# One load for the first keys, two banks for the last output tile, 28 accumulating transfers instead of 26, and all steps in a new order

## The chip, the core and the metric

The kernel runs on one core of one Trainium2 chip. A core has four engines that compute: TensorE (PE, matrix products; its weight loads are listed as PEld), VectorE (DVE), ScalarE (ACT) and GpSimd (POOL). SyncE (SP) only issues transfers. Each engine works through its own queue in the order of the program and waits on semaphores for the others. Transfers between memory and the core, and inside it, run on 16 DMA engines; they are issued here from SP's, ACT's and POOL's queues. The matrix products write into PSUM, eight banks of 128 x 512 floats; everything else lies in SBUF.

The metric is the device time of one execution in microseconds (us), as the median of several runs.

## The reference

Two stages. The first is attention without a softmax, for 4 batches of 4 heads, 1088 positions and a head size of 32. Queries and keys go through a feature map: two small matrices S1 and S2 give 8 numbers each, and the 64 products of these are the features. The second stage takes the 4352 rows of 128 numbers through a hidden layer of 2048 with a rational function in place of a usual activation.

```python
def phi(x):
    a = np.einsum('rd,bhsd->bhsr', S1, x)
    b = np.einsum('rd,bhsd->bhsr', S2, x)
    return np.einsum('bhsi,bhsj->bhsij', a, b).reshape(*x.shape[:-1], r * r)
q_p, k_p = (phi(q), phi(k))
kv = np.einsum('bhsf,bhsd->bhfd', k_p, v)
z = np.sum(k_p, axis=2)
num = np.einsum('bhsf,bhfd->bhsd', q_p, kv)
den = np.einsum('bhsf,bhf->bhs', q_p, z)[..., None] + 1e-06
x = (num / den)                    # then [B, S, H*D] as 4352 rows of 128
h = x @ w_in
P = a[0] + a[1] * h + a[2] * h2 + a[3] * h3      # h2 = h*h, h3 = h2*h
Q = 1.0 + np.abs(b[0]) * np.abs(h) + np.abs(b[1]) * h2
g = P / (Q + 1e-06)
out = g @ w_out
```

## The kernel before

The work is cut into steps, and the string `ORDER` (lines 38 to 76) lists all 650 of them by name. The loop at line 728 emits them in that order, so each engine's queue holds its share of the steps in that order and nothing is moved later. A step that stands earlier in the string than it needs to only matters on its own queue. A last letter of a step names the engine where there is a choice: `a` is ACT, `d` is DVE.

**Attention.** `I0` to `I11` (function `early`) are first loads, from SP's queue: in the kernel before, `I0` and `I1` bring the first batch's keys in two halves, `I11` brings S2, `I2` and `I7` the queries, `I3` the values, `I8` the coefficients, `I4` to `I6` w_in, `I9` and `I10` w_out. `F1.k`, `F1.q`, `F1.v` and so on load the next batches into the same buffers. `SS0` makes the sketch weights from S1 and S2 on DVE and POOL. `Kb` is the key part of batch b: `T0` to `T2` transposes on DVE, `s` sketches on PE, `c` a copy of them out of PSUM, `f` the features on DVE, `p` the products with the values on PE, `k` the copy of the result ("kvz"). `Qb.y` is chunk y of the queries of batch b: `T` transpose (DVE), `sk` sketch (PE), `c` copy, `dw` and `dr` a way through memory that repeats the sketches over the partitions (SP), `f` features (DVE), `p` products (PE), `pl` the denominator plus 1e-6, `r` reciprocal (DVE), `x` quotient (DVE), `b` transpose back (PE), `kk` copy into xT, the input of the second stage.

**Second stage.** 21 units, listed in `UNITS`, each some tokens by some of the 16 hidden blocks; most are 512 tokens by 8 blocks, which is a tile of 128 x 4096. Unit i has these steps: `H` h = w_in x on PE (line 518), in parts of 1024 columns into two wide PSUM buffers; `E` copies a part into SBUF as bf16 (line 272 on ACT); `U` takes |h| (DVE, line 531), `W` multiplies by |b1| and adds |b0| (line 539), `Y` multiplies by |h| (line 554). `L` and `X` on ACT make r = 1/Q as the exponential of minus a logarithm (lines 576 and 581). `P` is a3 h + a2 on DVE (line 559) or ACT (line 562), `V` multiplies it by h (line 572), `S` is s = h r (line 585), `G` multiplies the two (line 589). `Or`, `Os`, `Og` add r, s and g times the scaled w_out into the output tile in PSUM (line 618), each 32 products of 128 x 128 for a full unit: the constant, the linear and the higher terms of P. `ST` copies a finished output tile to SBUF, `OUT` stores it from SP's queue. The output copies have two buffers, so an `ST` needs the store of the tile two before it to have read.

Two lists change a unit's work. In units of `SQ`, ACT squares h (`D`) and an accumulating transfer from POOL's queue adds |h| to it in SBUF (`M`, line 550, two transfers of 2048 columns). In units of `TWO`, the linear coefficient is added to g by two accumulating transfers from POOL's queue (`A`, line 568, between `V` and `G`), and `Os` is left out. Units of `FOUR` (16 and 17) form the square and the cube on DVE (`B`, `C`) and have gathers `Om` and `On` in place of `Og`. `Zn` are n products of a zero tile that nobody reads, to keep PE at work.

**PSUM.** Three banks `att_ps` serve the attention, two buffers of two banks each serve `H`, and one bank, `out_ps`, holds the output tile (line 607). The first gather of a tile therefore needs the copy of the tile before to be done. The last tile, tokens 4096 to 4351, lies in one bank; its halves are copied by DVE (line 633) and by ACT (line 635) and stored from SP's and ACT's queues.

Of the kernel before, what the change touches and what calls it, by code (L numbers as in the profile page):

```python
# [43 lines left out]
Q0.1.b K1.p0 K1.p1 E2.1.a Q1.0.c.a w5.a Q0.1.kk.a L0.0 P2.0.d Q0.2.f Q0.2.p Q0.2.pl.a K1.k0.a X0.0 Q1.2.T U2.0.d
Q0.2.r Q1.1.sk Q1.2.sk Q0.3.dw F2.k Q1.0.dw Q0.2.x Q0.2.b Or0.0 W2.0.d S0.0 V2.0 K2.T0 G0.0 Y2.0 Q0.2.kk.a L1.0
Q1.1.c.a X1.0 H3.0 E3.0.a H3.1 E3.1.a K2.s0 K2.c0.a H3.2 L2.0 Q1.2.c.a E3.2.a F2.q Q0.3.dr Q1.1.dw S1.0 K2.T1 P3.0.d
G1.0 Q2.0.T K2.f0 Q2.1.T H3.3 E3.3.a Q0.3.f U3.0.d K2.T2 W3.0.d Q2.2.T Y3.0 Os0.0 H4.0 H4.1 Og0.0 Q2.0.sk Q1.0.dr
Q1.2.dw Q1.1.dr K2.s1 Q0.3.p X2.0 E4.0.a P3.1.a H4.2 Q0.3.pl.d K2.c1.d Q1.0.f Q2.0.c.a E4.1.a Og1.0 Q0.3.r V3.0 Q1.0.p
Q0.3.x L3.0 Q1.0.pl.a Q1.2.dr H4.3 E4.2.a Os1.0 Q1.0.r E4.3.a Q1.0.x Q0.3.b Q0.3.kk.a Q1.0.b Or2.0 S2.0 U4.0.d
Q1.0.kk.a H5.2 K2.f1 Q1.1.f W4.0.d X3.0 Q2.0.dw H5.3 E5.3.a G2.0 Q2.1.sk F2.v Q2.2.sk Q2.1.c.a F3.q E5.2.a Q1.1.p Y4.0  # L50
Q2.2.c.a Q1.1.pl.a Q1.1.r H5.0 E5.0.a Og2.0 L4.0 H5.1 Q1.2.f Or1.0 H6.2 Q1.1.x S3.0 E5.1.a Os2.0 ST2.a E6.2.a P4.0.d
Q3.1.T H6.3 Q1.1.b E6.3.a X4.0 Q1.1.kk.a H6.0 E6.0.a U5.0.d H6.1 Q3.0.T Q3.0.sk Q2.1.dw Q3.0.c.a W5.0.d E6.1.a K2.p0
K2.p1 K2.k0.a D6.0 Q1.2.p V4.0 Y5.0 S4.0 F3.k K3.T2 K3.T1 H7.0 K3.T0 E7.0.a U6.0.d G3.0 M6.0 Q1.2.pl.a Os4.0 H7.2
Or4.0 L5.0 E7.2.a H7.3 Q2.0.dr Q2.0.f Q2.0.p Q1.2.r Q2.1.dr Q2.1.f Q3.0.dw Q1.2.x X5.0 P5.0.d Q3.0.dr Q2.2.dw Q1.2.b
Q1.2.kk.a E7.3.a H7.1 Og3.0 G4.0 Q2.0.pl.d Q3.2.T E7.1.a Q2.0.r H8.3 V5.0 Q2.0.x Q2.0.b S5.0 L6.0 H8.2 E8.2.a U7.0.d
E8.3.a F3.v Or3.0 Q2.0.kk.a P6.0.d W7.0.d P7.0.d H8.0 V6.0 Os3.0 X6.0 Y7.0 E8.0.a S6.0 H8.1 E8.1.a U8.0.d D8.0 Q2.2.dr
OUT2 Og4.0 ST4.a H9.0 Q3.1.sk Q3.1.c.d Q2.2.f Q2.1.p Q2.1.pl.d K3.s0 K3.c0.d Q2.1.r Q3.2.sk Q3.2.c.d E9.0.a H9.1 Or6.0
L7.0 M8.0 Q2.1.x Q2.1.b K3.f0 H9.2 E9.1.a X7.0 E9.2.a Os6.0 H9.3 E9.3.a V7.0 AW0 Or5.0 P8.0.d H10.3 G6.0 L8.0 G5.0
S7.0 U9.0.d E10.3.a W9.0.d H10.0 E10.0.a V8.0 Q3.1.dw Y9.0 Og6.0 X8.0 H10.1 H10.2 Og5.0 E10.1.a A7.0 G7.0 E10.2.a
Q2.1.kk.a H11.0 Q3.1.dr Q3.1.f Os5.0 S8.0 D10.0 Q2.2.p E11.0.a U10.0.d P9.0.d K3.s1 Q2.2.pl.d ST6.a Q3.2.dw H11.1  # L60
Or8.0 Q3.0.f OUT6 Q2.2.r H11.2 K3.c1.d Q2.2.x L9.0 E11.1.a P10.0.d Q2.2.b K3.f1 V9.0 M10.0 V10.0 X9.0 E11.2.a H11.3
E11.3.a S9.0 K3.p0 K3.p1 w7.d U11.0.d w6.d L10.0 W11.0.d H12.1 E12.1.a Or7.0 H12.0 K3.k0.d Q3.0.p Q3.1.p X10.0 Y11.0
Q3.1.pl.d H12.2 Q3.0.pl.a G8.0 E12.0.a L11.0 E12.2.a Q3.0.r Os8.0 A9.0 H12.3 E12.3.a Q3.1.r Og8.0 Q3.0.x Q3.0.b Og7.0
Q3.1.x G9.0 Q2.2.kk.a S10.0 A10.0 Q3.0.kk.d H13.0 D12.0 Q3.1.b Q3.1.kk.a U12.0.d ST8.a M12.0 P12.0.d H13.1 E13.1.a
Q3.2.dr P11.0.d E13.0.a Or9.0 X11.0 H13.3 Q3.2.f V12.0 G10.0 V11.0 S11.0 H13.2 E13.3.a E13.2.a U13.0.d Or10.0 H14.1
E14.1.d L12.0 OUT4 Q3.2.p W13.0.d Q3.2.pl.a Q3.2.r H14.2 E14.2.d H14.0 X12.0 E14.0.a H14.3 Q3.2.x Q3.2.b Y13.0 E14.3.a
Q3.2.kk.a H15.2 D14.0 S12.0 U14.0.d A12.0 G12.0 E15.2.a Og10.0 Og9.0 ST10.a P14.0.d Z4 H15.3 P13.0.d L13.0 A11.0
Or12.0 G11.0 V14.0 V13.0 E15.3.a X13.0 S13.0 H15.1 Og11.0 E15.1.a H15.0 E15.0.a Or11.0 M14.0 U15.0.d L14.0 H16.1
# [11 lines left out]
def kernel(  # L80
# [61 lines left out]
    def spread_s(eng, i, s_in):  # L142
        t = consts.tile([128, D], FP, name=f"s_raw{i}")
        eng.dma_start(out=t, in_=bass.AP(tensor=s_in.tensor, offset=s_in.offset, ap=[[0, 16], [D, R], [1, D]]))
# [626 lines left out]
```

## Time and profile before

| | |
|---|---|
| median of 3 runs | 254.69 us (254.11 to 255.16) |
| the profiled execution | 254.41 us, span 252.6 us from first to last instruction |
| outside the span | 1.8 us |
| PE, DVE, ACT, POOL busy | 244.7, 240.3, 229.2, 31.2 us |
| granted TensorE clock | 1.00 |

The profile lists when each instruction of each engine started and how long it took, and for each idle time of an engine which event ended it. The busy share is an average over the span; the view by windows cuts it into stretches. Instructions on one engine overlap at their ends by up to about 0.1 us (a product of 128 x 4096 is listed with 2.28 us, and the next starts 2.20 us after it), and the ends of matrix products are modelled, so a PE that is listed as busy need not be at its peak.

### The profile page before, as it was taken

The numbers are of one execution on the slowest core, as the hardware profiler recorded it, in microseconds if no ns is written. First come the engines' busy times: TensorE is split into PE (matmuls) and PEld (weight loads), VectorE is DVE, ScalarE is ACT, GpSimd is POOL, SyncE is SP. The second block draws the span as 40 slices with busy tenths as digits, with TensorE's granted clock in tenths as the row PEclk, the third lists the DMA queues.
The fourth block names the chain that finished last, engine by engine and source line by source line (L and its number), as shares of the span: only waits on it lengthen the run. The fifth ranks groups of instructions, "written<-read, shape, count | busy, mean of one in ns | idle before, by whom it ended". The sixth has DMA issues, their size and how long they took to land.

```text
span 252.6 us, 6102 instructions
## 1 busy us (share of the span) xinstructions
PE 244.7 (97%) x2606; PEld 171.9 (68%) x2606; DVE 240.3 (95%) x231; ACT 229.2 (91%) x177; POOL 31.2 (12%) x59
## 2 busy tenths in 40 slices
...
GB/s 164 277 328 210 126 241 197 131 100 257 174 20 156 188 195 77 87 197 192 4 42 168 180 236 79 115 190 195 44 197 57 200 210 91 29 16 3 42 23 21
DMA packets 22458, 34.47 MB, mean 136 GB/s; under 512 B 2976, under 2 KB 14880, under 8 KB 22432
## 3 DMA queue, kind: packets, MB, share of 16 engines
...
## 4 chain that ended last, share of the span: by engine, by line
DVE 45%; PE 33%; issue 11%; DMA 6%; ACT 2%; SPq 1%; POOL 0%; DVEq 0%; ACTq 0%
PE h_ps L518 18%; PE out_ps L618 9%; DVE g L589 7%; DVE g L572 7%; DVE w L554 5%; DVE s L585 5%; DVE u L531 4%; DMA w<-u 4%; DVE g L559 4%; DVE w L539 3%; DMA v_sb<-in_v_dram 2%; PE att_ps L433 2%; DVE g L594 2%; PE att_ps L337 2%; DVE a_all L417 1%
## 5 line engine op out<-in xcount | busy, mean ns | idle before, releaser
L518 PE MATMUL h_ps<-xT,w_in_sb 128*128 128x512 f32 (+1 forms) x320 | 128.7, 539 | 0.1
L518 PEld LDWEIGHTS h_ps<-xT,w_in_sb 128*128 128x128 f32 x320 | 56.7, 190 | 36.6 <-issue 31.8
L272 ACT CAST hh<-h_ps 128x1024 bf16<-128x1024 f32 x66 | 66.6, 1047 | 3.3 <-PE h_ps L518 2.8
L581 ACT ACTIVATE r<-ln 128x4096 bf16<-128x4096 f32 (+2 forms) x21 | 63.1, 3005 | 0.4 <-ACT xT L272 0.3
L576 ACT ACTIVATE ln<-w 128x4096 f32<-128x4096 bf16 (+2 forms) x16 | 45.0, 2811 | 0.4 <-DVE w L554 0.4
L585 DVE TENSOR_TENSOR s<-hh,r 128x4096 bf16<-128x4096 bf16 (+2 forms) x21 | 39.5, 1881 | 0.0
L618 PEld LDWEIGHTS <-r 128*128 128x128 bf16 x544 | 31.8, 98 | 8.9 <-issue 8.6
L618 PEld LDWEIGHTS <-g 128*128 128x128 bf16 x544 | 31.6, 98 | 6.9 <-issue 6.0
L618 PE MATMUL out_ps<-w_out,r 128*128 128x128 bf16 x544 | 33.6, 219 | 1.2 <-ACT out_sb L272 1.1
L589 DVE TENSOR_TENSOR g<-g,s 128x4096 bf16<-128x4096 bf16 (+2 forms) x19 | 34.7, 1835 | 0.0
L572 DVE TENSOR_TENSOR g<-g,hh 128x4096 bf16<-128x4096 bf16 (+2 forms) x19 | 34.6, 1829 | 0.0
L618 PE MATMUL out_ps<-w_out,g 128*128 128x128 bf16 x480 | 29.7, 219 | 0.0
L554 DVE TENSOR_TENSOR w<-w,u 128x4096 bf16<-128x4096 bf16 (+2 forms) x16 | 28.0, 1750 | 0.0
L550 POOL DMA_DIRECT2D w<-u x10 | 9.3, 1026 | 131.0 <-ACT w L544 111.6
L618 PEld LDWEIGHTS <-s 128*128 128x128 bf16 x352 | 20.6, 98 | 4.7 <-issue 4.6
L531 DVE TENSOR_SCALAR u<-hh 128x4096 uint16<-128x4096 uint16 (+2 forms) x21 | 21.4, 1020 | 0.8 <-ACT hh L272 0.8
L568 POOL DMA_DIRECT2D g<-ones x16 | 16.8, 1452 | 26.2 <-DVE g L572 8.6
L544 ACT ACTIVATE w<-hh,root 128x4096 bf16<-128x4096 bf16 x5 | 18.9, 3773 | 0.0
L576 ACT ACTIVATE ln<-w,scale 128x4096 f32<-128x4096 bf16 x5 | 18.9, 3771 | 0.0
L559 DVE TENSOR_SCALAR g<-hh,a_k 128x4096 bf16<-128x4096 bf16 (+2 forms) x16 | 18.6, 1174 | 0.0
L618 PE MATMUL out_ps<-w_out,s 128*128 128x128 bf16 x288 | 18.0, 219 | 0.0
L539 DVE TENSOR_SCALAR w<-u,b_abs 128x4096 bf16<-128x4096 bf16 (+2 forms) x15 | 16.6, 1107 | 0.1
...
## 6 DMA issues: line engine op xcount, KB each, us to landing
g<-ones POOLq DMA_DIRECT2D x16, 512.0 KB, 10.4
...
```

Source lines behind the costliest of these rows:

```text
L272: nc.scalar.copy(out=out, in_=in_)
L518: nc.tensor.matmul(t[:, (x - part * m) * tl:(x - part * m + 1) * tl], lhsT=w_in_sb[:, (f0 + x) * 128:(f0 + x + 1) * 128], rhs=xT[:, p:p + ...
L531: nc.vector.tensor_scalar(out=at(i, "u", *c).bitcast(U16), in0=at(i, "hh", *c).bitcast(U16), scalar1=0x7FFF, scalar2=None, op0=AX.bitwise_and)
L539: nc.vector.tensor_scalar(out=at(i, "w", *c), in0=at(i, "u", *c), scalar1=ab1, scalar2=ab0, op0=AX.mult, op1=AX.add)
L554: nc.vector.tensor_mul(out=at(i, "w", *c), in0=at(i, "w", *c), in1=at(i, "u", *c))
L559: nc.vector.tensor_scalar(out=at(i, "g", *c), in0=at(i, "hh", *c), scalar1=a3, scalar2=a2, op0=AX.mult, op1=AX.add)
L572: nc.vector.tensor_mul(out=at(i, "g", *c), in0=at(i, "g", *c), in1=at(i, "hh", *c))
L576: nc.scalar.activation(out=ln_sb[:, :ce - c], in_=at(i, "w", c, ce), func=ACT.Ln, bias=1.0 + 1e-6, scale=scale0 if i in SQ else 1.0)
L581: nc.scalar.activation(out=at(i, "r", c, ce), in_=ln_sb[:, :ce - c], func=ACT.Exp, scale=-1.0)
L585: nc.vector.tensor_mul(out=at(i, "s", *c), in0=at(i, "hh", *c), in1=at(i, "r", *c))
L589: nc.vector.tensor_mul(out=at(i, "g", *c), in0=at(i, "g", *c), in1=at(i, "s", *c))
L618: nc.tensor.matmul(outs[t0][:, m * 128:(m + 1) * 128], lhsT=z[:, m * 128:(m + 1) * 128], rhs=w, start=first and j == 0 and m == 0, stop=le ...
```

## The change

1. **First keys.** `I0` becomes one contiguous load of all 34 rows per partition (`load_k(0)`), `I1` is gone. S2 (`I11`) is loaded from POOL's queue instead of SP's, ahead of everything else on POOL. `SS0` stands before `K0.T0` on DVE's queue. `F1.k` stands before `I8`, `I6` before `I5`, and `I10` behind `Q0.2.dr`.
2. **Output tiles.** The last tile is two tiles in two of the `att_ps` banks, one for each 128 tokens; a gather fills the first and then the second. The tiles of tokens 3328 and 3840 (units 15 to 17, list `LATE`) lie in `att_ps` banks too.
3. **Transfers.** Unit 8 joins `TWO`: `Os8.0` goes, `A8.0` comes.
4. **Engines.** From DVE to ACT: `K0.k0`, `K1.c1`, `K2.c1`, `K3.c0`, `K3.c1`, `Q0.3.c`, `Q3.1.c`, `Q3.2.c`, `Q0.1.pl`, `Q0.3.pl`, `Q2.1.pl`, `P0.0`. From ACT to DVE: `Q0.0.c`, `K1.k0`, `Q0.2.pl`, `Q1.0.pl`, `Q1.2.pl`, `Q3.0.pl`, `Q3.2.pl`.
5. **Idle products.** `Z10 Z3 Z3 Z2 Z4` become `Z10 Z1 Z1`.
6. **Order.** All steps are listed anew; below are the beginning, the stretch from `V7.0` to `G9.0`, and the end. On SP's queue the stores now go 4, 2, 6, 8, 12, 10, 16, 14, 17, 20 (before: 2, 6, 4, 8, 10, 12, 14, 16, 17, 20).

```diff
-TWO = (7, 9, 10, 11, 12, 13, 14, 15)
+TWO = (7, 8, 9, 10, 11, 12, 13, 14, 15)
+LATE = (15, 16, 17)
...
-I0 I11 I1 I2 K0.T0 SS0 Z10 K0.s0 K0.T1 K0.T2 K0.c0.a K0.f0 Q0.0.T Z3 K0.s1 Z3 Q0.0.sk I3 K0.p0 I8 F1.k I7 I9 I4 I5
-K0.c1.a K0.f1 Q0.0.c.a Q0.0.f Q0.1.T K0.p1 K0.k0.d Q0.2.T K1.T0 Q0.1.sk Q0.0.p Q0.2.sk K1.s0 K1.T1 Q0.1.c.a Q0.0.pl.a
-Q0.0.r Q0.0.x K1.T2 Q0.2.c.a Z2 Q0.0.b K1.s1 I6 I10 Q0.2.dw Q0.1.f K1.c0.a Q0.3.T Q0.0.kk.a H0.0 w2.d K1.f0 AB0 RT0
-w0.a KA0 KA1 KA2 w4.a K1.c1.d F1.q K1.f1 E0.0.a U0.0.d H1.0 Q0.3.sk E1.0.a F1.v Q0.2.dr Q0.1.p H2.0 P0.0.d Q0.3.c.d
...
+I0 SS0 I2 Z10 Z1 K0.T0 I3 K0.s0 K0.T1 K0.c0.a K0.T2 Q0.0.T I7 K0.f0 F1.k K0.s1 Z1 K0.c1.a K0.f1 Q0.0.sk Q0.2.T K0.p0
+K0.p1 I8 K0.k0.a AB0 Q0.1.T Q0.1.sk Q0.1.c.a Q0.0.c.d Q0.0.f Q0.0.p Q0.0.pl.a Q0.2.sk Q0.2.c.a I9 K1.T2 RT0 K1.T1
+K1.s1 K1.T0 Q0.0.r KA0 KA1 KA2 Q0.0.x I4 Q0.0.b K1.c1.a K1.s0 Q0.0.kk.a w4.a I6 Q0.1.f Q0.3.T Q0.1.p H0.0 Q0.1.pl.a
+K1.c0.a w2.d I5 H1.0 Q0.2.dw K1.f1 w0.a F1.v Q0.1.r E0.0.a P0.0.a Q0.1.x F1.q Q0.1.b Q0.2.dr E1.0.a K1.f0 U0.0.d
...
+Q2.2.f P8.0.d M8.0 K3.f0 V7.0 Q3.1.c.a L7.0 Q3.1.dw G6.0 V8.0 E9.1.a X7.0 A7.0 H9.3 S7.0 E9.3.a E9.2.a U9.0.d L8.0
+Or5.0 H10.3 Q2.1.b Q2.1.kk.a OUT4 H10.0 G5.0 W9.0.d Og6.0 P9.0.d E10.3.a E10.0.a X8.0 H10.2 E10.2.a G7.0 Y9.0 H10.1
+S8.0 Os5.0 Q3.1.dr E10.1.a D10.0 U10.0.d H11.0 Og5.0 P10.0.d E11.0.a ST6.a Q2.2.p Q2.2.pl.d A8.0 M10.0 G8.0 Q2.2.r
+K3.s1 Q3.1.f Q2.2.x H11.3 H11.1 K3.c1.a L9.0 K3.f1 V9.0 A9.0 OUT2 V10.0 Or8.0 E11.3.a E11.1.a Q3.2.dw Q3.2.dr X9.0
+S9.0 H11.2 E11.2.a U11.0.d H12.1 K3.p0 K3.p1 K3.k0.d W11.0.d H12.0 A10.0 L10.0 Or7.0 w7.d Q3.1.p Y11.0 Q3.0.p
+Q3.0.pl.d E12.1.a E12.0.a Q3.1.pl.d w6.d Q3.0.r X10.0 Q3.1.r H12.3 Q3.0.x E12.3.a G9.0 H12.2 E12.2.a Q2.2.b Q2.2.kk.a
...
-L18.0 On16.0 ST16.a U19.0.d H20.0 OUT14 W19.0.a P19.0.d B17.0 V19.0 Or17.0 C17.0 X18.0 Y19.0 P18.0.a V18.0 OUT16
-E20.0.a U20.0.d Os17.0 S18.0 L19.0 W20.0.d X19.0 Om17.0 On17.0 S19.0 ST17.a Y20.0 Or18.0 Or19.0 Os19.0 Os18.0 G19.0
-P20.0.a G18.0 Og19.0 Og18.0 L20.0 X20.0 Or20.0 V20.0 OUT17 S20.0 G20.0 Os20.0 Og20.0 ST20 OUT20
+P19.0.d B17.0 V19.0 Om16.0 C17.0 Or17.0 L18.0 W19.0.a Y19.0 ST16.a OUT16 P18.0.a V18.0 Os17.0 X18.0 Om17.0 E20.0.a
+U20.0.d On17.0 L19.0 X19.0 Or18.0 ST17.a OUT14 S18.0 Or19.0 W20.0.d S19.0 Os19.0 Y20.0 G19.0 Os18.0 Og19.0 G18.0
+P20.0.a V20.0 Og18.0 L20.0 X20.0 Or20.0 OUT17 S20.0 G20.0 Os20.0 Og20.0 ST20 OUT20
...
-    s_raw = [spread_s(nc.scalar, 0, S1)]
+    s_raw = [spread_s(nc.scalar, 0, S1), spread_s(nc.gpsimd, 1, S2)]
...
-        if n == 11:
-            s_raw.append(spread_s(nc.sync, 1, S2))
-        elif n < 2:
-            j, e = ((0, 4), (4, NT))[n]
-            nc.sync.dma_start(out=k0.rearrange("p (m t d) -> p m t d", m=NM, d=D)[:, :, j:e],
-                              in_=bass.AP(tensor=k.tensor, offset=k.offset + j * D,
-                                          ap=[[NJ * D, 128], [NT * D, NM], [1, (e - j) * D]]))
+        if n == 0:
+            load_k(0)
...
         if first:
-            outs[t0] = ops.tile([128, TC], FP, name="out_ps")
+            if t0 + tl == n_tok:
+                outs[t0] = [att.tile([128, 512], FP, name="end_ps", tag="att_ps") for m in range(2)]
+            elif i in LATE:
+                outs[t0] = att.tile([128, TC], FP, name="end_ps", tag="att_ps")
+            else:
+                outs[t0] = ops.tile([128, TC], FP, name="out_ps")
         c, ce = span(i, "LSGGG"[y], k)
+        if t0 + tl == n_tok:
+            left[t0] -= (ce - c) // tl
+            for m in range(2):
+                for j, x in enumerate(range(c // tl, ce // tl)):
+                    x0 = x * tl + m * 128
+                    z = live[i]["s3", 0][:, x0:x0 + 128] if y == 4 else at(i, "rsgg"[y], x0, x0 + 128)
+                    nc.tensor.matmul(outs[t0][m][:, :128], lhsT=z, rhs=w_sb[y][:, f0 + x, :], start=first and j == 0,
+                                     stop=left[t0] == 0 and j == (ce - c) // tl - 1)
+            return
...
-        nc.vector.tensor_copy(out=o[:, 0:128], in_=outs[t0][:, 0:128])
+        nc.vector.tensor_copy(out=o[:, 0:128], in_=outs[t0][0][:, :128])
         last = live[i]["o2"] = mid.tile([128, 128], FP, name="last", bufs=1)
-        nc.scalar.copy(out=last, in_=outs[t0][:, 128:256])
+        nc.scalar.copy(out=last, in_=outs[t0][1][:, :128])
```

56 lines of the change are left out of this document (25 added, 31 removed).

## The prediction

> **What bounds the kernel now.** I start with the page for the busy totals, and then take the windows, because an average over stages with different limits says little.
>
> ```profile
> span 252.6 us, 6102 instructions
> ...
> PE 244.7 (97%) x2606; PEld 171.9 (68%) x2606; DVE 240.3 (95%) x231; ACT 229.2 (91%) x177; POOL 31.2 (12%) x59
> ```
>
> ```profile
> core 0: us, PE busy (x) PEld busy (x) DVE busy (x) ACT busy (x) POOL busy (x), PEclk, DMA share, GB/s
> 0.00:20.60 20.60, 18.69 (x238) 12.54 (x238) 13.35 (x27) 8.08 (x18) 5.03 (x33) 1.00 0.93 259
> 20.60:103.00 82.40, 81.44 (x797) 51.68 (x793) 81.68 (x93) 79.18 (x71) 1.98 (x2) 1.00 0.56 153
> 103.00:243.00 140.00, 138.78 (x1491) 102.34 (x1487) 139.91 (x104) 138.51 (x87) 24.17 (x24) 1.00 0.58 116
> 243.00:252.60 9.60, 5.76 (x96) 5.33 (x95) 5.34 (x9) 3.45 (x4) 0.00 (x0) 1.00 0.10 27
> ```
>
> Read the windows by subtraction. DVE idles 20.60 − 13.35 = 7.25 us at the head, 0.72 in the next 82.4, 0.09 in the next 140, 4.26 at the end. PE looks the busiest in the total, but some of that is products that nobody reads; in the two middle windows it idles 0.96 and 1.22, ACT 3.22 and 1.49. So for 222 us all three are nearly full, and DVE is fullest. A gain must come from DVE's work, from its idle head, or from the tail, and PE and ACT have to keep up. The list of waits shows what ended DVE's idle time:
>
> ```profile
> DVE k_p L299 <- DMA k_sb<-in_k_dram: 3.7, 2, 2.7
> ...
> ACT last L635 <- DVE out_sb L633: 2.5, 1, 2.5
> ...
> PE out_ps L618 <- ACT out_sb L272: 1.1, 1, 1.1
> ...
> DVE kvz L274 <- PE att_ps L337: 1.1, 1, 1.1
> ...
> DVE u L531 <- ACT hh L272: 0.8, 1, 0.8
> ```
>
> (Columns: total us, times, longest.) The largest one is the first keys. The chain that ended last goes through DVE in the middle, for example these (start, us, engine):
>
> ```profile
> 85.88 1.79 PE out_ps L618 x32
> ...
> 142.45 1.14 DVE u L531
> ...
> 144.25 1.26 DVE w L539
> ...
> 165.19 2.20 DVE g L572
> ```
>
> The sum is made against the profiled execution, 252.6 us of span and 1.8 outside it, 254.41 in all. That is 0.28 below the median of the runs shown; I predict for the median without a correction.
>
> **The change part by part: work moved between DVE and ACT.** The groups, with different shapes kept apart, give the prices (busy us, mean ns of one):
>
> ```profile
> L562 ACT ACTIVATE g<-hh,a_k 128x1024 bf16<-128x1024 bf16 x2 | 2.5, 1240 | 0.0
> ...
> L445 ACT ACTIVATE den<-att_ps 128x12 f32<-128x12 f32 x5 | 1.1, 229 | 0.0
> L559 DVE TENSOR_SCALAR g<-hh,a_k 128x1024 bf16<-128x1024 bf16 x2 | 1.1, 543 | 0.0
> ...
> L197 PE MATMUL att_ps<-idle 128*128 128x512 bf16 x4 | 1.0, 379 | 0.0
> ...
> L274 DVE COPY b_sk<-att_ps 128x160 f32<-128x160 f32 x3 | 0.9, 294 | 0.0
> L442 DVE TENSOR_SCALAR den<-att_ps 128x12 f32<-128x12 f32 x5 | 0.8, 167 | 0.0
> ...
> L274 DVE COPY sk_sb<-att_ps 128x176 f32<-128x176 f32 x2 | 0.6, 322 | 0.3 <-PE att_ps L373 0.3
> L274 DVE COPY xT<-att_ps 128x384 f32<-128x384 f32 x1 | 0.6, 551 | 0.0
> ```
>
> DVE loses the four key copies `K1.c1`, `K2.c1`, `K3.c0`, `K3.c1` (4 × 0.294), the three query copies `Q0.3.c`, `Q3.1.c`, `Q3.2.c` (3 × 0.322), three `pl` (3 × 0.167) and `P0.0` (0.543): 3.2 us. It gains five `pl` (0.84) and `Q0.0.c`, a copy of 128x512 that no row has on DVE; the copy of 128x384 takes 0.551, so I take 0.70 (between 0.55 and 0.9). `K0.k0` and `K1.k0` change places and cancel. **First term: −1.7 us**, all on the path, as DVE has no idle there. ACT takes P at 1.24 for DVE's 0.54; with copies at about DVE's prices and `pl` at 0.229 it gains some 4.0 and sheds 1.7. These 2.3 net lie beside DVE's work, in ACT's 3.22 + 1.49 = 4.7 us of idle time in the middle windows. Without that cover they cost 2.3 in full.
>
> **The head.** The first rows in time (start, us, what, and the idle before it with what ended it):
>
> ```profile
> 0.72 0.45 SPq L167 DMA_DIRECT2D k_sb<-in_k_dram  x1
> ...
> 1.24 0.67 SPq L144 DMA_DIRECT2D s_raw<-in_S_dram  x1
> ...
> 1.95 0.59 SPq L167 DMA_DIRECT2D k_sb<-in_k_dram  x1
> ...
> 3.79 0.71 DVE L299 STREAM_TRANSPOSE k_p<-k_sb 128x512 f32<-128x512 f32 x1 [2.67 <-DMA k_sb<-in_k_dram]
> ...
> 4.43 0.26 DVE L225 STREAM_TRANSPOSE sT<-s_raw 128x32 f32<-128x32 f32 x2
> ...
> 6.01 0.84 DVE L299 STREAM_TRANSPOSE k_p<-k_sb 128x384 f32<-128x384 f32 x2 [1.01 <-DMA k_sb<-in_k_dram]
> ...
> 16.18 3.72 PE L518 MATMUL h_ps<-xT,w_in_sb 128*128 128x256 f32 x16
> ...
> 19.60 1.91 ACT L272 CAST hh<-h_ps 128x1024 bf16<-128x1024 f32 x2
> 20.62 0.43 DVE L531 TENSOR_SCALAR u<-hh 128x1024 uint16<-128x1024 uint16 x1 [0.78 <-ACT hh L272]
> ```
>
> DVE idles 3.5 us before 3.79 and 3.75 after it, 1.0 of that for the second half of the keys, 1.1 for kvz and 0.8 for the first u. The half issued at 0.72 is there at 3.79, the other, issued at 1.95, at 6.01. A single load at 0.72 cannot land before 3.8; twice the bytes behind no S2 on SP's queue should land before 6.0. I take 4.7. DVE makes the sketch weights (4.43 to about 5.0, 0.55 us) while it waits, so it idles some 3.9 before the first transpose and never again for keys. That needs S2 early: on POOL it goes ahead of the memsets, which shift by under 1 us and are read only by the first query sketch, now at about 7.3. An S2 that came as late as the quickest accumulating transfer lands (5.5 us after issue, row below) would be there at 6.2. Of the other waits I keep 0.9, since the steps are interleaved otherwise and the first h is nearer: SP sheds two issues, so the values go out about 1.3 us earlier. `F1.k`, which overwrites the key buffer, now makes SP wait for `K0.T2`, with `I8`, `I9`, `I4`, `I6`, `I5` behind it; that transpose ends at about 6.3 (6.85 before), so w_in's first part still goes out earlier and H0.0 can start at some 15.6 in place of 16.18. `I10` (w_out) moves behind `Q0.2.dr`, and its first reader, w1, w3 or w5, stands at about 27 us: covered. The price of that cover gone is the landing of one load, 2 to 3 us. **Second term: 4.8 in place of 7.25, −2.5 us** (bounds: −4.3 with the keys at 3.8 and no later wait; −0.2 with the keys at 6.0 and 1.1 more waits). U0.0 then starts near 18.8: the head also holds 0.4 us more of the moved copies and some 0.3 of steps drawn forward.
>
> **The tail.**
>
> ```profile
> 248.13 0.62 PE L618 MATMUL out_ps<-w_out,g 128*128 128x128 bf16 x8
> ...
> 248.79 0.29 DVE L633 COPY out_sb<-out_ps 128x128 f32<-128x128 f32 x1 [0.71 <-PE out_ps L618]
> ...
> 249.12 0.27 ACT L635 COPY last<-out_ps 128x128 f32<-128x128 f32 x1 [2.49 <-DVE out_sb L633]
> ```
>
> ACT's copy waits for DVE's, as both read one bank; in two banks it starts with the last product at about 248.8. The first bank is also done 4 products before the second (4 × 0.056 = 0.22). **Third term: −0.3** (0 to −0.6). The 1.1 us that PE waited on the output copy goes too, as the late tiles no longer share a bank with the one before; DVE's G20 is late next, so this counts as nothing. `ST17` now needs the store 14, which SP issues behind store 16: a near tie, 0 to 0.5.
>
> **PE and the transfer.** `Os8.0` (the row of 32 products at 85.88 prices it at 1.79) and Z4 (1.0) leave PE, both behind 100 us; some 6 us of idle products leave the head, where they hid behind DVE. A8.0 asks for two more issues on POOL, 0.17 busy in the third window.
>
> **New idle of DVE.** Up to 103 us DVE would be ahead by 2.5 + 1.7, less 0.3 for a copy that ran at 104: 3.9. But PE's work up to there is the same; it can be ahead only by its earlier start (0.6) and its old idle time (0.96), 1.6. PE makes the h that DVE reads, so DVE would wait 3.9 − 1.6 = 2.3. Behind 103, PE sheds 2.8 and DVE almost nothing, so it doesn't grow. It lies between 0 (gathers, which nobody is in haste for, stand later in the new order and let h pass) and 4.2 (ACT's 2.3 in that stretch too). **Fourth term: +2.3**, the middle, from the PE window.
>
> Sum: 254.4 − 1.7 − 2.5 − 0.3 + 2.3 = **252.2 us**.
>
> **The rivals.**
> *Full cover.* The order lets PE postpone gathers, DVE never waits: 254.4 − 4.5 = 249.9. For it: in the third window DVE idles 0.09 beside a PE with 1.22. Against: PE's 0.96 before 103.
> *ACT becomes the bound.* ACT's old idle stays (it waits for E's h and for w) and its 2.3 us more are added, where DVE's gain is lost: 254.4 − 2.5 − 0.3 + 0.7 of the head + 2.3 = 254.6, no change. For it: 138.51 of 140.
> *The head gains nothing.* Keys at 6.0 or S2 at 6.2, then the sketch weights on the path: 254.4 − 0.2 − 0.3 − 0.1 = 253.8; DVE's shed work is still limited by PE.
> *The other side: accumulating transfers land late.* Where A of a unit has not landed, G stands on DVE's queue and everything behind it.
>
> ```profile
> L568 POOL DMA_DIRECT2D g<-ones x16: 860/1064/3832, 108.9 to 200.8; - x16
> ...
> DMA to landing us min/median/max: 5.5/10.4/14.3
> ```
>
> The first row has the issue times in ns. From V to G of a unit, the new order leaves on DVE's queue 11.6 us in unit 9 (V10, S9, U11, W11, Y11 and small steps, by 2.20, 1.14 and 1.26), 12.5 in unit 7 and 17 or more in the others. At the longest landing seen, 14.3, with an issue of 1.06 (15.4), G9 waits 3.8 and G7 2.9: +6.7 in place of the 2.3, 254.4 − 4.5 + 6.7 = 256.6 us. At the median, 10.4 + 1.06 = 11.5, nobody waits; the two waits eat up the 4.5 at a landing of 13.2 (2 × 14.3 − 24.1), and it decides from there on. Against it: no wait for such a transfer is among DVE's now.
>
> [...]
>
> **How the numbers follow.** Chances: forecast (250.9 to 253.1) 0.44, full cover 0.16, ACT 0.20, head 0.06, late transfers 0.14. The range takes in the full cover and the ACT case with 0.6 beyond: 249.6 to 255.6; outside are late transfers in full and gains over 4.8. The forecast's own range is 250.9 to 253.1. What can be told from no change is 0.5%, 1.3 us: the forecast and full cover are faster (0.60), ACT, head and the weak end of the forecast the same (0.23), late transfers and the strong end of the ACT case slower (0.17).
>
> **What would show it.** Right: the first key transpose near 4.7 with the sketch weights ahead of it and no second key wait; U0.0 at 18 to 19.5; DVE busy near 238.7, PE near 236 to 238 and ACT near 231.5; no wait of ACT's last copy on DVE's; DVE idle of 2 to 3 us on h before 103. Wrong: a key load at 6; a wait of DVE at L589 on a transfer from `ones`; ACT with under 1 us of idle in a window and DVE waiting on it.

## The result, and the profile after

The changed kernel takes 256.32 us (median of 13 runs, 254.18 to 258.31); the kernel before took 254.69 (254.02 to 255.45). The ratio is 1.0061, 95% interval 1.0033 to 1.0089: slower by 0.6%. The prediction was 252.2, with a range of 249.6 to 255.6, and the result lies above that range. The runs of the changed kernel also spread over 4.1 us, those of the kernel before over 1.4. Ratios, here and below, leave out runs over 1.5% above the fastest of their kernel; here these are two of the 13 (258.17 and 258.31). The profiled execution took 257.82 us, 1.5 above its median; its span is 256.0, against 252.6 before.

The page of the changed kernel, and its windows (the last columns are granted clock, DMA share and GB/s):

```profile
span 256.0 us, 6008 instructions
...
PE 243.9 (95%) x2564; PEld 171.7 (67%) x2564; DVE 239.4 (94%) x226; ACT 230.5 (90%) x182; POOL 30.9 (12%) x62
```

```profile
0.00:20.60 20.60, 17.66 (x217) 12.02 (x218) 12.02 (x25) 6.17 (x18) 5.32 (x34) 1.00 0.66 197
20.60:60.00 39.40, 37.56 (x360) 24.34 (x359) 37.16 (x54) 37.02 (x41) 0.00 (x0) 1.00 0.70 194
...
103.00:150.00 47.00, 46.20 (x488) 30.91 (x485) 45.71 (x34) 46.69 (x33) 11.38 (x12) 1.00 0.74 158
```

The same two later windows in the kernel before:

```profile
20.60:60.00 39.40, 38.44 (x373) 24.09 (x368) 38.93 (x57) 37.14 (x43) 0.00 (x0) 1.00 0.58 166
...
103.00:150.00 47.00, 47.00 (x528) 31.54 (x524) 46.96 (x40) 47.00 (x30) 8.77 (x10) 1.00 0.70 141
```

DVE's work fell by only 0.9 us (240.3 to 239.4) and its idle time grew by 4.3 (252.6 − 240.3 = 12.3 before, 256.0 − 239.4 = 16.6 after): by 1.3 in the first 20.6 us (8.58 against 7.25), by 1.8 up to 60 (2.24 against 0.47), by 1.25 between 103 and 150 (1.29 against 0.04). The list of waits says for what (total us, times, longest):

```profile
DVE sT L221 <- DMA s_raw<-in_S_dram: 4.9, 2, 3.9
...
DVE rec L446 <- ACT den L441: 1.7, 2, 1.1
...
DVE a_all L413 <- DMA b_all<-sk_d: 0.6, 1, 0.6
...
DVE q_sb L362 <- DMA q_sb<-in_q_dram: 0.6, 1, 0.6
```

The wait for the keys is gone, and a longer one for the sketch matrices S1 and S2 (`s_raw`) stands in its place. DVE's first rows (start, us), and its first u:

```profile
5.03 0.21 DVE L221 STREAM_TRANSPOSE sT<-s_raw 128x32 f32<-128x32 f32 x1 [3.92 <-DMA s_raw<-in_S_dram]
6.25 0.21 DVE L221 STREAM_TRANSPOSE sT<-s_raw 128x32 f32<-128x32 f32 x1 [1.01 <-DMA s_raw<-in_S_dram]
...
6.61 1.43 DVE L295 STREAM_TRANSPOSE k_p<-k_sb 128x512 f32<-128x512 f32 x3
...
22.67 0.42 DVE L527 TENSOR_SCALAR u<-hh 128x1024 uint16<-128x1024 uint16 x1
```

The first u starts at 22.67, where the kernel before had 20.62 and the prediction 18.8. PE shows a second effect. First its rows after, then the same steps of the kernel before:

```profile
1.17 4.87 PE L193 MATMUL out_ps<-idle 128*128 128x512 bf16 x11 [1.17 <-DVE idle L186]
7.37 2.19 PE L302 MATMUL h_ps<-S,k_p 128*64 128x64 f32 x36 [1.32 <-DVE k_p L295]
...
10.21 2.08 PE L379 MATMUL h_ps<-ln,SAB 64*128 64x256 f32 x8
```

```profile
1.18 3.70 PE L197 MATMUL out_ps<-idle 128*128 128x512 bf16 x10 [1.18 <-DVE idle L190]
5.06 0.69 PE L306 MATMUL h_ps<-S,k_p 128*64 128x64 f32 x16 [0.18 <-DVE S L229]
...
6.64 0.80 PE L306 MATMUL h_ps<-S,k_p 128*64 128x64 f32 x20
...
8.45 1.13 PE L383 MATMUL h_ps<-ln,SAB 64*128 64x256 f32 x8 [0.25 <-DVE ln L366]
```

The 36 sketch products of the first keys took 2.19 us after and 0.69 + 0.80 before, the first query sketch 2.08 and 1.13. PE was slow here, though the granted clock is listed as 1.00 in both windows.

### The profile page after: what moved, and what is told of

It reads as the page before. It is cut to its first block, busy times and chain, and to the rows that moved or that the text cites. A ratio compares the mean times of both kernels' runs of the same rounds, so it can differ in the third digit from the quotient of the medians.

```text
span 256.0 us, 6008 instructions
## 1 busy us (share of the span) xinstructions
PE 243.9 (95%) x2564; PEld 171.7 (67%) x2564; DVE 239.4 (94%) x226; ACT 230.5 (90%) x182; POOL 30.9 (12%) x62
## 4 chain that ended last, share of the span: by engine, by line
ACT 41%; DVE 16%; DMA 15%; issue 14%; PE 12%; POOL 1%; SPq 0%; ACTq 0%; DVEq 0%; POOLq 0%
ACT r L577 13%; ACT hh L268 12%; DMA w<-u 9%; ACT ln L572 7%; ACT w L540 7%; PE h_ps L514 5%; DVE w L550 4%; DMA b_all<-sk_d 3%; DVE g L585 2%; DMA s_raw<-in_S_dram 2%; DVE g L590 2%; DVE s L597 2%; DVE s L581 1%; DVE u L527 1%; DMA sk_d<-sk_sb 1%
## 5 line engine op out<-in xcount | busy, mean ns | idle before, releaser
L628 PEld LDWEIGHTS <-r 128*128 128x128 bf16 x512 | 29.8, 98 | 7.0 <-issue 6.5
L628 PEld LDWEIGHTS <-g 128*128 128x128 bf16 x512 | 29.9, 98 | 6.0 <-issue 5.5
L628 PE MATMUL out_ps<-w_out,r 128*128 128x128 bf16 x416 | 25.5, 219 | 0.0
L628 PE MATMUL out_ps<-w_out,g 128*128 128x128 bf16 x416 | 25.5, 219 | 0.0
L564 POOL DMA_DIRECT2D g<-ones x18 | 15.9, 1045 | 31.4 <-DVE g L568 17.0
L628 PEld LDWEIGHTS <-s 128*128 128x128 bf16 x288 | 16.8, 98 | 3.5 <-issue 2.6
L540 ACT ACTIVATE w<-hh,root 128x4096 bf16<-128x4096 bf16 x5 | 18.8, 3756 | 0.0
L429 PE MATMUL att_ps<-kvz,a_all 128*64 128x66 f32 x288 | 10.9, 224 | 1.6 <-DVE a_all L413 1.4
```

What stands on the lines that cost most here:

```text
L540: nc.scalar.activation(out=at(i, "w", *c), in_=at(i, "hh", *c), func=ACT.Square, scale=root)
L628: nc.tensor.matmul(outs[t0][:, m * 128:(m + 1) * 128], lhsT=z[:, m * 128:(m + 1) * 128], rhs=w, start=first and j == 0 and m == 0, stop=le ...
```

## The experiments

Four runs of one chip share the runs of the kernel before, so the ratio to it is what is compared, also between chips. "New" below is the changed kernel. The theories are: 1, the sketch weights are late; 2, the order behind the first u loses time; 3, ACT has become the bound; 4, single steps moved to ACT are late there; 5, PE with its h holds the stretch (a rival of 4); 6, the second queries stand behind the second values; 7, PE works slowly behind an idle stretch.

**The first loads.** S2 back on SP's queue in the new kernel:

```diff
-    s_raw = [spread_s(nc.scalar, 0, S1), spread_s(nc.gpsimd, 1, S2)]
+    s_raw = [spread_s(nc.scalar, 0, S1)]      # and I11 (S2, SP's queue) behind I0
```

> The changed kernel with S2 loaded from SP's queue right behind the single key load, as I11, in place of POOL's queue; nothing else differs. Theory 1 (the sketch weights, first on DVE's queue, wait for S2 from POOL until 6.25 us, and the head carries it on): S2 is there with S1 at about 5.0, the wait of 1.0 us goes, U0.0 starts at about 21.7 in place of 22.67 and the median is 255.3. Theory 2 (the loss lies in the order behind the first u): U0.0 may move, but the time stays within 0.5 us of 256.3. Theory 3 (ACT has become the bound through the steps moved to it): the same as theory 2.

Median 255.0, ratio 1.0005 (0.9978 to 1.0031). S2 came at 5.53 (S1 at 4.64), the first sketches took 1.27 us, the first u started at 19.91. That is earlier than theory 1 expected (21.7); the time fell by 0.56% of 254, 1.4 us. The profiled execution is the slowest of the twelve, 257.13, in spite of its early first u: what makes executions of the new order differ lies, here at least, behind the head.

All the old first loads in the new kernel:

```diff
-I0 SS0 I2 Z10 Z1 K0.T0 I3 K0.s0
+I0 I11 I1 I2 Z10 Z1 K0.T0 SS0 I3 K0.s0      # I0, I1: the keys in two halves
```

> The changed kernel with the first loads as in the kernel before: keys in two halves, S2 between them on SP's queue, the sketch weights behind the first key transpose; the rest of the new order stays. Theory 1 (the head's loss is the late sketch weights): first key transpose at 3.8, U0.0 at 20.0 to 20.7 in place of 22.67, median 254.3 (2 us less). Theory 2 (order behind the first u): median 255.8 or more. Theory 3 (ACT): 255.8 or more.

Median 254.47, ratio 0.9999 (0.9972 to 1.0027): 0.62% less than the new kernel, 1.6 us. The first u started at 19.92. So the loads explain the whole loss against the kernel before, but what was meant to be gained is missing too: the rest of the change is worth nothing that can be told from zero.

The new first loads in the kernel before:

```diff
-I0 I11 I1 I2 K0.T0 SS0 Z10 K0.s0
+I0 SS0 I2 K0.T0 Z10 K0.s0      # one key load, S2 from POOL's queue
```

> The kernel before with only the first loads of the change: one key load, S2 from POOL's queue, the sketch weights ahead of the first key transpose; order, engines and tiles as before. Theory 1: the sketch weights at 6.2 in place of 4.4, U0.0 at 22 to 22.7 in place of 20.62, median 256.3 to 256.7. Theories 2 and 3: within 0.7 us of 254.7.

Median 258.14, ratio 1.0144 (1.0114 to 1.0173), 3.6 us and more than theory 1 expected. Its first u started at 24.91, 4.3 late, although the weights were only 2.1 late (6.51 against 4.43). In the old order the same loads cost over twice as much as in the new one.

The old head with the new order behind it:

```diff
-I0 SS0 I2 Z10 Z1 K0.T0 I3 ... E1.0.a K1.f0 U0.0.d Q0.1.kk.a I10 W0.0.d
+I0 I11 I1 I2 K0.T0 SS0 Z10 ... K1.f1 E0.0.a U0.0.d Q0.1.p Q0.1.pl.a H1.0
```

> The old head joined to the new order: loads and all steps up to the first U as the kernel before lists them (with their old engines), then the remaining steps in the new order, with new engines, the two banks and the 28 transfers; without idle products behind the joint. Theory 1: U0.0 at 20.6 and from there as the changed kernel or better, median 254.3 or less. Theory 2: U0.0 at 20.6, but DVE still idles about 1.8 us between 20.6 and 60 and about 1.3 between 103 and 150, and the median is 255.5 to 256.5. Theory 3: DVE waits on r, hh and the sketch copies of ACT, ACT idles less than 3 us between the first u and the last, 255.5 or more.

Median 254.8, ratio 1.0022 (1.0000 to 1.0044), between what theory 1 expected (254.3 or less) and theory 2 (255.5 to 256.5). The first u started at 20.08, and behind it DVE waited again: 1.05 us up to 60, 2.03 between 60 and 103, all of that for one reciprocal (below), and 0.15 between 103 and 150. Theory 2 had 1.8 in the first of these stretches and 1.3 in the last. So a loss behind the head is at the edge of the noise here, and its place is a single wait.

**The loads one at a time, in the kernel before.**

```diff
-I0 I11 I1 I2 K0.T0 SS0      # two halves, S2 between them
+I0 I11 I2 K0.T0 SS0         # one load, S2 behind it on SP's queue
```

> The kernel before with the keys in one load, S2 behind it on SP's queue and the sketch weights behind the first key transpose; nothing else. It shows when one load lands and what it does to S1 and S2. If the single load is harmless (the loss is S2 on POOL's queue alone): first key transpose at 4.7, the weights right behind it, ratio 0.995 to 1.001. If the single load by itself delays the keys and both sketch matrices: first key transpose at 5.3 or later, ratio 1.003 to 1.007, with S2 on POOL bringing the rest of the 1.0144 of b_loads.

```profile
4.50 0.71 DVE L296 STREAM_TRANSPOSE k_p<-k_sb 128x512 f32<-128x512 f32 x1 [3.38 <-DMA k_sb<-in_k_dram]
5.14 0.17 DVE L222 STREAM_TRANSPOSE sT<-s_raw 128x32 f32<-128x32 f32 x1
5.51 0.21 DVE L222 STREAM_TRANSPOSE sT<-s_raw 128x32 f32<-128x32 f32 x1 [0.21 <-DMA s_raw<-in_S_dram]
```

Ratio 1.0018 (1.0007 to 1.0028). The single load is there at 4.50, and S2 at 5.5 where two halves had let it be there by 4.43: here the small transfer landed 1.1 us or more later behind the large one.

```diff
-I0 I11 I1 I2 K0.T0 SS0
+I0 I1 I2 K0.T0 SS0          # and S2 from POOL's queue
```

> The kernel before with S2 from POOL's queue and nothing else: keys in two halves, the sketch weights behind the first key transpose. With b_loads (1.0144) and b_onekey (1.0018) it splits the loss of the first loads. If POOL's queue by itself makes S2 late: the sketch weights at 5.8 or later in place of 4.43, ratio 1.006 to 1.013. If it is the crowd of the single key load that makes both sketch matrices late: weights at 4.6 or earlier, ratio 0.996 to 1.002.

Ratio 1.0007 (0.9984 to 1.0030). S2 was there at 5.04. Each of the two alone costs little, 0.25% in sum. In b_loads, S2 comes at 6.5 and the loss is 1.44%; but b_loads also has the weights ahead of the first key transpose. What remained open was whether it is this place of the weights or PE.

```diff
-I0 SS0 I2 K0.T0 Z10         # b_loads
+I0 I2 K0.T0 SS0 Z10
```

> b_loads (ratio 1.0144) with the sketch weights behind the first key transpose on DVE's queue; Z10 as in the kernel before. If the place of the weights ahead of the transposes is what costs (the transposes, 1.4 us, then run behind S2's landing and PE goes idle longer): first key transpose at 4.5, the first sketches about 0.8 us earlier, ratio 1.004 to 1.010. If S2's landing alone decides: weights at 6.2 to 6.5 all the same, ratio above 1.011.

DVE's and PE's rows:

```profile
5.38 0.71 DVE L294 STREAM_TRANSPOSE k_p<-k_sb 128x512 f32<-128x512 f32 x1 [4.26 <-DMA k_sb<-in_k_dram]
...
1.18 4.45 PE L192 MATMUL out_ps<-idle 128*128 128x512 bf16 x10 [1.18 <-DVE idle L185]
7.32 0.69 PE L301 MATMUL h_ps<-S,k_p 128*64 128x64 f32 x16 [1.69 <-DVE S L224]
```

Ratio 1.0060 (1.0030 to 1.0090). The keys came at 5.38 (4.5 was expected, and 4.50 measured in b_onekey) and S2 at 6.82, as late as in b_loads, and yet more than half of the loss was gone. PE is at its usual speed in this execution (0.69 for the first sketches), though it stood idle for 1.69. The 12 times lie in two clusters of six, 255.55 to 256.08 and 257.25 to 258.55. The mean granted clock, which is listed for each execution, goes with them: 0.996 to 1.000 in the lower six, 0.990 to 0.993 in five of the upper six (0.998 in the sixth). That fits a PE that is slow in some executions; only one, of the lower cluster, was profiled. The listed clock is no price by itself, though: in b_loads the three runs near 257.6 have 0.990 to 0.992 and the three near 258.7 have 0.998.

```diff
-I0 SS0 I2 K0.T0 Z10         # b_loads
+I0 SS0 I2 K0.T0 Z15
```

> b_loads (the kernel before with the first loads of the change, ratio 1.0144) with Z15 in place of Z10. Theory 7: the first sketches take 0.69 in place of 1.12, the three idle products behind them 0.82 in place of 1.46, U0.0 starts near 22.3 in place of 24.91, ratio 1.006 to 1.008. Rival (the late weights alone): U0.0 stays above 24, ratio 1.013 to 1.016.

Five more products that nobody reads, and nothing else. PE's rows of b_loads, and then with Z15:

```profile
1.18 4.45 PE L192 MATMUL out_ps<-idle 128*128 128x512 bf16 x10 [1.18 <-DVE idle L185]
7.62 1.12 PE L301 MATMUL h_ps<-S,k_p 128*64 128x64 f32 x16 [2.00 <-DVE k_p L294]
8.68 1.46 PE L192 MATMUL out_ps<-idle 128*128 128x512 bf16 x3
```

```profile
1.18 5.20 PE L192 MATMUL out_ps<-idle 128*128 128x512 bf16 x15 [1.18 <-DVE idle L185]
7.74 0.69 PE L301 MATMUL h_ps<-S,k_p 128*64 128x64 f32 x16 [1.37 <-DVE k_p L294]
8.36 0.82 PE L192 MATMUL out_ps<-idle 128*128 128x512 bf16 x3
```

Ratio 1.0054 (1.0037 to 1.0072), where theory 7 had 1.006 to 1.008 and the rival 1.013 or more; the first u at 22.39. The weights came no earlier (6.63). All 12 runs (256.17 to 256.98) lie below all six of b_loads (257.57 to 258.77). So of the 3.6 us of b_loads about 2.3 (0.90% of 254) are a slow PE; the rest is left to the late loads. Why PE is slow there, no run shows. What the rows show: ten idle products took 4.45 us, and 3.70 in the kernel before, where PE worked on after 0.18; in b_loads it then stood idle for 2.00 and the next products took 1.6 to 1.8 times as long (1.12 against 0.69, 1.46 against 0.82). An idle time alone doesn't do it: in a_s2_sp, where eleven idle products took 3.84, it was 1.63 and the 36 sketches took 1.27. Nor do both together in every execution: in b_loads_t0 the ten took 4.45 as well, the idle time was 1.69, and the sketches took 0.69. The listed clock doesn't show it either: it is 1.00 in the head of the changed kernel, whose products are slow too. Later windows of a_loads_eng and b_engines, below, do list 0.50 behind idle stretches of PE.

The same in the new kernel:

```diff
-I0 SS0 I2 Z10 Z1 K0.T0 ... K0.s1 Z1
+I0 SS0 I2 Z15 K0.T0 ... K0.s1 Z3
```

> The changed kernel with more idle products and nothing else: Z15 in place of Z10 Z1 ahead of the first sketches, Z3 in place of Z1 behind the second. The late sketch weights stay. Theory 7 (PE stood idle for 1.32 us before the late sketches and then worked at about half its speed until 15 us: 2.19 us for 36 sketch products that take 0.69 + 0.80 in the kernel before, 2.08 for the first query sketch that takes 1.13): PE works at its speed, those two take about 1.3 and 1.13, U0.0 starts near 21 in place of 22.67, ratio 1.000 in place of 1.0061 and the runs spread less than the 4.1 us of the changed kernel. Rival (the loss of the head is the wait for S2 alone, PE's speed is hidden): ratio 1.005 to 1.007.

```profile
7.75 1.27 PE L301 MATMUL h_ps<-S,k_p 128*64 128x64 f32 x36 [0.96 <-DVE k_p L294]
...
10.14 1.14 PE L378 MATMUL h_ps<-ln,SAB 64*128 64x256 f32 x8 [0.38 <-DVE k_p L313]
```

Ratio 1.0039 (1.0015 to 1.0064), the runs within 2.7 us. PE was at its speed and the first u at 21.02, 1.65 earlier, as theory 7 has it; the ratio lies between theory 7 (1.000) and its rival (1.005 to 1.007). The time followed by a third of the 1.65, and the intervals of 1.0039 and 1.0061 overlap. In this execution DVE waited 1.53 for a reciprocal and 0.94 for an accumulating transfer, so a part of the gain was lost later.

The listed clocks show more than the times. In 8 of the 13 executions of the changed kernel the mean granted clock was 0.984 to 0.993; in a_z it was 0.997 or more in all 12, and in the kernel before 0.996 or more in every run beside these experiments. So with the idle products of a_z the listed clock stayed up. The profiled execution of the changed kernel, with 1.00, isn't one of the 8; where the clock fell in those, no trace shows.

**Steps on other engines.** The 19 steps on their new engines, at their places in the old order (for instance):

```diff
-K0.k0.d ... K1.c1.d ... P0.0.d Q0.3.c.d ... Q2.1.pl.d ... K3.c1.d
+K0.k0.a ... K1.c1.a ... P0.0.a Q0.3.c.a ... Q2.1.pl.a ... K3.c1.a
```

> The kernel before with only the 19 steps on their new engines, at their old places in the order. The prediction's first term (1.7 us of work off DVE, all on the path, ACT's 2.3 more covered): DVE busy 238.6 and the ratio to before 0.993 to 0.995. Theory 4 (what is moved to ACT then waits in ACT's queue and DVE waits for it): DVE busy 238.6, but its idle time grows by 1.5 us or more at reciprocals, features and quotients behind steps of ACT, and the ratio is 0.999 or above.

Median 259.97, ratio 1.0218 (1.0189 to 1.0246). DVE busy 239.7 in place of 240.3, but idle 259.2 − 239.7 = 19.5 us, 7.2 more: features waited 1.81 behind a copy on ACT, P of unit 3 2.73 and P of unit 2 1.00 for copies of h on ACT, two reciprocals 1.6 in sum. The 2.73 is not ACT's queue alone. PE's rows, and the same step in the kernel before:

```profile
33.43 6.07 PE L518 MATMUL h_ps<-xT,w_in_sb 128*128 128x512 f32 x8
```

```profile
31.03 3.70 PE L518 MATMUL h_ps<-xT,w_in_sb 128*128 128x512 f32 x8
```

PE had stood idle for 1.76, 0.70 and 0.63 us between 27.5 and 32.1, the first of these for a copy into xT on ACT, and from 32 to 38 us its granted clock is listed as 0.50 (last section). ACT's copies of h then waited 1.89 and 1.33 for PE. So a part of the 5.5 us is a slow PE behind a late copy; the run doesn't separate the two.

The opposite, the old engines in the new order (on a_loads):

```diff
-K0.k0.a ... Q0.0.c.d ... Q2.1.pl.a ... Q3.2.pl.d
+K0.k0.d ... Q0.0.c.a ... Q2.1.pl.d ... Q3.2.pl.a
```

> a_loads (the changed kernel with the old first loads, ratio 0.9999) with the 19 moved steps back on their old engines, at their new places. The prediction's first term (moving them takes 1.7 us off the path): DVE busy rises by 1.6 and the ratio is 1.004 to 1.007. Theory 4 (what is moved to ACT makes DVE wait for ACT, so the moves give nothing): DVE busy rises by 1.6, its idle time falls by as much or more, ratio 0.994 to 1.001.

Median 265.15, ratio 1.0416 (1.0385 to 1.0448), 10.6 us more than a_loads; the first u starts at 25.20, 5.3 later. DVE busy rose by 2.2 (241.3) and its idle time by 6.8 (14.9 to 21.7). Two of the waits:

```profile
15.01 0.69 DVE L420 TENSOR_TENSOR a_all<-h_ps,a_all 128x512 f32<-128x512 f32 x1 [2.42 <-ACT a_all L273]
...
171.58 0.23 DVE L451 RECIPROCAL rec<-den 128x12 f32<-128x12 f32 x1 [2.08 <-ACT den L446]
```

`Q0.0.c`, back on ACT, stands behind `Q0.1.c` there; `Q3.2.pl`, back on ACT, behind a square and a logarithm of 3.7 us each and a copy between them. Here too PE's listed clock fell, behind the wait at 15.01:

```profile
15.75 1.15 PE L434 MATMUL att_ps<-kvz,a_all 128*64 128x66 f32 x16 [1.89 <-DVE a_all L420]
...
19.51 0.69 PE L434 MATMUL att_ps<-kvz,a_all 128*64 128x66 f32 x16
```

```profile
16.00:18.00 2.00, 2.00 (x38) 2.00 (x38) 1.69 (x5) 0.81 (x5) 0.48 (x3) 0.50 0.02 8
```

The same 16 products took 1.15 and then 0.69, and the granted clock is 0.50 in the window of the first. Neither the first term nor theory 4 forecast this run: in the new order the moves save 10.6 us, in the old order they cost 5.5. In this kernel a step's engine has no price of its own apart from its place in that engine's queue and from what waits behind it, PE and its clock included.

One of the moves is wrong in its new place also. ACT's and DVE's rows of the changed kernel around 104 us:

```profile
102.20 1.93 ACT L268 CAST hh<-h_ps 128x1024 bf16<-128x1024 f32 x2
103.99 0.33 ACT L268 COPY sk_sb<-att_ps 128x176 f32<-128x176 f32 x1
104.19 0.22 ACT L441 ACTIVATE den<-att_ps 128x12 f32<-128x12 f32 x1
```

```profile
104.44 0.23 DVE L446 RECIPROCAL rec<-den 128x12 f32<-128x12 f32 x1 [1.13 <-ACT den L441]
```

`Q2.1.pl` went to ACT and stands there behind E8.1, E8.0 and a copy; DVE does nothing until it is through. Back on DVE, on top of a_loads:

```diff
-Q2.1.pl.a
+Q2.1.pl.d
```

> The changed kernel with the old first loads (as in a_loads) and, beside them, the one denominator Q2.1.pl back on DVE. Theory 4 (a moved step waits in ACT's queue: Q2.1.pl stands there behind the two copies E8.1 and E8.0 and a sketch copy, and DVE's reciprocal waits 1.13 to 2.03 us for it at about 102 us): that wait is gone, DVE's idle time between 60 and 103 falls below 0.5, and the ratio to before is about 0.996 where a_loads has 0.9999 (1.0 us less). Rival 5 (something else holds the stretch, PE with its h): the reciprocal no longer waits, but as much idle time shows up at the next step of DVE, and the ratio stays 0.998 to 1.002.

```profile
60.00:103.00 43.00, 42.40 (x432) 27.18 (x431) 42.97 (x39) 41.43 (x28) 1.97 (x2) 1.00 0.46 119
```

Median 253.67, ratio 0.9980 (0.9966 to 0.9993). The wait is gone (DVE idle 0.03 in this window, 1.23 in a_loads), and the median ratio fell by 0.5 us of the 1.0 expected, though the interval overlaps that of a_loads. It is the only version whose interval lies below 1, by 0.2%. It still waited 1.57 us for the second batch's queries at 24.3:

```diff
-F1.v Q0.1.r E0.0.a P0.0.a Q0.1.x F1.q
+F1.q F1.v Q0.1.r E0.0.a P0.0.a Q0.1.x
```

> a_loads_pl (old first loads, Q2.1.pl on DVE, ratio 0.998) with the second queries' load F1.q ahead of the second values' F1.v on SP's queue, as in the kernel before. Theory 6 (DVE's wait of 1.57 us at 24.3 for these queries is their place behind the values): the load is issued about 2 us earlier, the wait falls below 0.5, ratio 0.994. Rival: the transfers are held up by the crowd on the DMA engines and not by the queue, the wait stays above 1 us or another one on the values takes its place, ratio 0.997 to 0.999.

That wait went, and the profiled execution took 252.8 us, but the median is 254.05, the ratio 0.9973 (0.9944 to 1.0002) and the runs spread from 252.5 to 257.0: not told apart from a_loads_pl.

The same with as many idle products up to the second sketches as the kernel before:

```diff
-Z10 Z1 ... K0.s0 ... K0.s1 Z1          # a_fq
+Z10 ... K0.s0 Z3 ... K0.s1 Z3
```

> a_fq (old first loads, Q2.1.pl on DVE, second queries ahead of the second values; ratio 0.9973 with runs from 252.5 to 257.0) with three idle products behind the first sketches and three behind the second, as many as the kernel before has there. Theory 7 (the spread of the new order is PE that in some executions falls to half its speed in the head, for want of idle products): spread below 2 us, ratio 0.993 to 0.996. Rival (the spread comes from transfers): spread stays above 3 us, ratio 0.997.

Ratio 0.9989 (0.9954 to 1.0023), runs from 252.94 to 257.0. Theory 7 doesn't explain the spread of the new order where the loads are the old ones. The clocks say the same: 0.997 or more in all 12 runs here. What does explain it stays open.

**Tail and transfers.** Only the output tiles of the change, in the kernel before:

```diff
-            outs[t0] = ops.tile([128, TC], FP, name="out_ps")
+            if t0 + tl == n_tok:
+                outs[t0] = [att.tile([128, 512], FP, name="end_ps", tag="att_ps") for m in range(2)]
+            elif i in LATE:
+                outs[t0] = att.tile([128, TC], FP, name="end_ps", tag="att_ps")
...
```

> The kernel before with only the output tiles of the change: the last tile in two banks, the tiles of units 15 to 17 in banks of the attention. The prediction's third term: ACT's last copy starts with the last product and no longer behind DVE's, PE's wait of 1.1 us on the output copy is gone, the ratio is 0.998 to 1.000. Rival: the freed PE time before 243 us moves the end forward by up to 1.1 us, ratio 0.995.

```profile
248.66 0.29 DVE L648 COPY out_sb<-end_ps 128x128 f32<-128x128 f32 x1 [0.49 <-PE end_ps L621]
248.88 0.27 ACT L650 COPY last<-end_ps 128x128 f32<-128x128 f32 x1 [2.17 <-PE end_ps L621]
```

Ratio 0.9993 (0.9978 to 1.0009). Against 248.79 and 249.12 the copies start 0.13 and 0.24 earlier and no longer one behind the other, and PE's wait on the output copy is gone. The forecast of 0.3 fits; the interval holds no change as well.

Only the two more transfers, with `Os8.0` left to them:

```diff
-TWO = (7, 9, 10, 11, 12, 13, 14, 15)
+TWO = (7, 8, 9, 10, 11, 12, 13, 14, 15)
...
-ST6.a Q3.2.dw ... G8.0 E12.0.a L11.0 E12.2.a Q3.0.r Os8.0
+ST6.a A8.0 Q3.2.dw ... G8.0 E12.0.a L11.0 E12.2.a Q3.0.r
```

> The kernel before with unit 8 in TWO: the 32 products Os8.0 go, the accumulating transfers A8.0 come, between OUT6 and the next transfers on POOL's queue. The prediction: PE loses 1.8 us of work behind 100 us, where it isn't the bound, no wait of DVE on the transfers, ratio 0.998 to 1.001. The rival of late transfers: the two more issues push those of units 9 and 10 back, DVE waits at a G for a transfer by over 1 us, ratio 1.004 or more.

Ratio 0.9993 (0.9974 to 1.0011), PE busy 1.4 less, no wait of DVE on an accumulating transfer. In a_loads there was one, at G7:

```profile
124.74 2.29 DVE L590 TENSOR_TENSOR g<-g,s 128x4096 bf16<-128x4096 bf16 x1 [1.26 <-DMA g<-ones]
```

The longest landing there was 14.6 us. The transfers of unit 7, with the short lead that the prediction counted, are late in three of the nine profiles of the new order (1.26, and 0.94 in a_z and 0.33 in a_s2_sp), and not in that of the changed kernel.

## Why the prediction was wrong

*Where DVE's time lies.* Right: DVE was idle in head and tail alone, and every loss found is new idle time of DVE.

*First term, −1.7 for work moved off DVE.* Wrong. By its rows the sum was near (DVE busy 0.6 to 1.6 less in the runs with the moves, 0.9 in the changed kernel), but the step "all on the path, as DVE has no idle there" failed: the waits that a moved step brings or saves are several times its own duration (b_engines 5.5 us slower, a_loads_eng 10.6 slower than a_loads). One such wait, 1.13 to 2.03 us for `Q2.1.pl`, is larger than all the `pl` moved. It could be read off the order: the three steps ahead of it on ACT's queue. Nor did the term count that a late copy lets PE stand idle and then work slowly, as in b_engines (1.76, 0.70 and 0.63 us idle, then 6.07 for eight products that take 3.70 in the kernel before).

*Second term, −2.5 in the head.* Wrong, the largest miss: the first u came 2.05 later, not 1.8 earlier. The single key load, taken as 4.7, came at 4.50 with S2 behind it on SP's queue, but at 5.38 with S2 on POOL's queue as in the change (b_loads_t0). S2 was missed by more: 6.25, which is the upper bound given (6.2), and S1 on ACT's queue came late too, at 5.03. Both were treated as hidden behind the keys because each was bounded by itself; nothing in the sum had the small transfers land behind a 544 KB load that is issued first. The rival "the head gains nothing", 253.8 with a chance of 0.06, had this mechanism but no loss in it.

*The idle products.* Two things were wrong. That "some 6 us of idle products leave the head" is a misreading: the head had 18 of them, 5.9 us in all, and the change keeps 12 (5.5 us in its profile). So PE busy was 243.9, where 236 to 238 was forecast; in a_loads, where PE is at speed, it was 240.4. And they were costed at nothing, as they "hid behind DVE". Taking out six did cost nothing where the loads were the old ones (a_loads has its first u at 19.92, and a_fq_z, which puts four back, gained nothing that can be told). But with the late loads PE's speed hung on them: five more were worth about 2.3 us in the old order (b_loads against b_loads_z), and in the new kernel, with two more behind the second sketches, 1.65 us at the first u. The sum had no term for PE's speed at all.

*Third term, the tail, and the transfer.* Right in mechanism and within what can be measured: 0.1 to 0.2 us in the profile.

*Fourth term, +2.3 of new idle.* The cause was wrong, and the size near only by luck. In a_loads, whose head is like the old one, DVE idles 2.7 us more between 20.6 and 103 (3.40 against 0.72), where the term had 2.3, and another 1.2 up to 150, where it had none. The waits are queries 1.25, repeated sketches 0.74, a reciprocal 1.23 and a transfer 1.26. None of the larger ones is a wait for h, and up to 103 PE idles too (3.10 us). The forecast let PE hold DVE back; what held it back were single operands from a queue or a transfer.

The rival of late transfers was at work once in a while and not the cause: its 256.6 is the number nearest to the 256.3 measured, but by luck, since DVE waits for no accumulating transfer in the changed kernel's profile. ACT as a bound isn't shown either (ACT idles 5.2 us between 20.6 and 246 in the new profile, 4.7 between 20.6 and 243 before). The range's upper end is also not what it says: 0.6 beyond the ACT case (254.6) is 255.2, not 255.6.

In short, the 4.1 us between forecast and result are some 1.6 of the first loads (a_loads against the changed kernel) and 2.5 of a gain that is missing with the old loads too. The first part is shown by runs; for the second, the waits that took DVE's gain are read from single executions. Only those of `Q2.1.pl` and of the second queries were taken away (a_loads_pl, a_fq), and most of the gain stayed missing.
